# A gated mix of full and windowed attention on one core: shifted copies in place, four quads under way, and a new planner table

## The chip, the cores and the metric

The kernel runs on one core of a Trainium2 chip. The metric is the device time of one execution in microseconds (us); the median of three runs of the kernel before is 827.52 us. The core has five engines that work side by side, each through its own instructions in a fixed order, with semaphores between them: TensorE (PE in the profile) multiplies matrices, VectorE (DVE), ScalarE (ACT) and GpSimd (POOL) work on elements, and SyncE (SP) starts most transfers.

## The reference, cut to what matters

```python
x = A_x                                        # 1 x 2048 x 640, bf16
g = sigmoid((x * gate_w).sum(-1, keepdims=True))
# A: full attention, 32 heads of 20 columns
p = softmax(einsum("bhqd,bhkd->bhqk", q, k) * 20 ** -0.5)
a = einsum("bhqk,bhkd->bhqd", p, v)            # heads side by side, then @ A_wo
# B: each query sees 8 keys, at distances 0, 2, ..., 14
b = ...                                        # softmax over the 8, values, @ B_wo
return g * a + (1 - g) * b
```

q, k and v of A and of B are x times their own 640 x 1920 weights. The exponentials of A are the large work: 32 heads of 2048 x 2048 scores.

## The kernel before, in words

**Units, groups, tiles.** A *unit* is the scores of one head for 128 keys and 512 queries. A *group* is four heads (j = 0 to 3) and 512 queries, so 64 units, and there are 32 groups. Units come in *tiles*, numbered s. `next_tile` (L1472) puts two units in a tile, in one of two double-buffered score tensors, and a third if the third bank of that score tensor is free. That bank (x = 1 + s % 2) is also one of the three banks (`BANKS`, L342) in which all other PE work leaves its results, called `side`. `qk(s)` (L1511) makes the scores, with four heads in the four row strips of the array; `exp(s)` (L1544) lets ScalarE take the exponential of the two or three units into one of five buffers `ebuf`; `pv` (L1556) multiplies them by the values, four at a time in the four column strips, and adds up in one accumulator, `obank`, which serves one group after another. When a group's units are all added, `close` (L1635) starts its normalization (`gen_norm`).

**Rides and quads.** ScalarE doesn't take every unit. A unit can *ride* in the third place of a tile to VectorE, which makes a bit pattern of its exponential by arithmetic on integers (L1537: add an offset, clamp at 0, write int16, which is read as bf16). Four units of one key block, one of each head of a group, are a *quad*. To be exact enough, a quad is used four times, k = 0 to 3: as it is, and with 32, 64 and 96 added to its integers (`SHIFTS`, L48; the shift is L806), each time with values that have been multiplied by another weight (`WEIGHTS`; POOL does it once for a quad, L798, into `vS`). So a quad has four *slices*, and each slice has one value matmul for each head (L1592). In this kernel the quads lie in two buffers `uD`, and the shifted copies in a ring of three, `eD`.

**The planner.** All instructions are placed when the kernel is built. `_Sched.task` (L188) appends an instruction to its engine's list and charges it a duration; an engine's list runs in that order on the chip, and the charges decide only the order. A charge for signals (`LAT`) and one for a change between row strips and column strips (`SWITCH`) are added. The main loop (L1699 to 1753) makes for each tile s: scores, exponential, perhaps value matmuls (`pv_slot`, L1653), and then, in `spend`, side work until shortly before the charged end of the exponential before (`SLACK`). Side work is written as generators that ask for PE time, VectorE time or a bank, each with a priority (`step`, L1150): projections of q, k, v, the window attention of B (`gen_bproj`, `gen_b`), normalization, output (`gen_fold`), and the shifts (`gen_d`, L789). Where PE has too little to do, `filler` (L1599) adds matmuls on zeros or into a free bank.

**What holds rides and shifts back.** `wanted` (L1398) opens a quad only if its `uD` buffer is free, if no more than two quads have slices left, if VectorE's charged backlog is small, and if the group has at least `DTIME` left; a ride is taken only if the backlog is under `DWAIT`. `gen_d` shifts one quad after another, and only when a place of the ring is free. Slices are taken in order of quads and of k, up to three (`NS`) at a visit of `pv_slot`; it is visited at every second tile, or when two slices are ready. At a group's end `pv_slot` forces what is missing.

`PLAN` (L50) sets 18 such numbers anew from given tiles on. The pace of B is given by constants (`BT0`, `BT1`, `BALL`, `XT0`, `XT1`), which the change doesn't touch.

Of the kernel before, what the change touches and what calls it, by code (L numbers as in the profile page):

```python
# [50 lines left out]
    0: ((0.3, 0.64), 0.31, 2.5, 2.5, 0.49, -1.34, -0.1, 11.8, 7.0, 8.15, 0.52, 0.47, 4.4, 4.0, 0.0, 0.71, 2, 0.0),  # L51
    10: ((0.3, 0.64), 0.31, 2.5, 2.5, 0.66, -1.34, -0.1, 11.8, 7.0, 8.15, 0.52, 0.47, 4.4, 4.0, 0.0, 0.71, 2, 0.0),
    20: ((0.3, 0.64), 0.31, 2.5, 2.5, 0.49, -1.34, -0.83, 11.8, 7.0, 8.15, 0.52, 0.47, 4.4, 4.08, 0.0, 0.71, 2, 0.0),
    30: ((0.32, 0.68), 0.31, 2.5, 5.5, 0.94, -1.34, -0.83, 11.8, 7.0, 7.65, 0.52, 0.47, 4.4, 5.28, 0.0, 0.73, 2, 0.0),
    40: ((0.32, 0.68), 0.3, 2.5, 5.5, 0.94, -1.34, -0.83, 11.8, 7.0, 8.82, 0.52, 0.47, 4.4, 5.28, 0.0, 0.73, 2, 1),
    50: ((0.32, 0.81), 0.3, 2.5, 5.5, 0.94, -1.34, -0.83, 11.8, 7.0, 8.82, 0.52, 0.47, 4.4, 5.28, 0.0, 0.73, 2, 1),
    60: ((0.32, 0.68), 0.31, 2.5, 5.5, 0.94, -1.34, -0.83, 11.8, 6.7, 7.65, 0.52, 0.64, 4.4, 4.34, 0.0, 0.73, 2, 0),
    70: ((0.32, 0.68), 0.3, 2.5, 5.5, 0.94, -1.5, -0.83, 11.8, 5.5, 8.82, 0.52, 0.47, 4.76, 5.28, 0.0, 0.73, 2, 1),
    80: ((0.29, 0.82), 0.3, 2.5, 5.5, 0.94, -1.34, -0.83, 11.8, 7.0, 8.82, 0.52, 0.47, 4.4, 5.28, 0.0, 0.73, 2, 1),
    90: ((0.29, 0.82), 0.06, 2.5, 6.6, 0.95, -1.34, -0.83, 11.59, 7.0, 8.82, 0.52, 0.47, 4.4, 5.28, 0.0, 0.73, 2, 0),  # L60
    100: ((0.32, 0.68), 0.31, 2.5, 5.5, 0.94, -1.34, -0.83, 11.8, 7.0, 7.03, 0.52, 0.47, 4.4, 4.3, 0.0, 0.69, 2, -3),
    110: ((0.32, 0.68), 0.31, 2.5, 5.5, 0.94, -1.49, -0.5, 11.8, 7.0, 6.64, 0.52, 0.47, 4.4, 4.3, 0.0, 0.66, 2, -3),
    120: ((0.32, 0.68), 0.31, 5.5, 5.5, 0.94, -1.15, -0.5, 9.67, 7.0, 6.64, 0.52, 0.47, 4.4, 3.98, 0.0, 0.66, 2, -3),
    130: ((0.32, 0.68), 0.31, 2.5, 5.5, 0.82, -1.6, -0.5, 11.8, 7.0, 6.64, 0.52, 0.44, 4.4, 4.54, 0.0, 0.66, 2, 0),
    160: ((0.31, 0.76), 0.33, 2.5, 1.0, 0.82, -1.6, -0.34, 11.8, 7.0, 6.64, 0.61, 0.44, 4.4, 4.12, 0.0, 0.66, 2, 0),
    180: ((0.31, 0.76), 0.28, 2.5, 1.0, 0.72, -1.6, -0.5, 11.8, 5.5, 6.64, 0.52, 0.44, 4.4, 3.94, 0.0, 0.66, 2, 0),
    190: ((0.31, 0.76), 0.28, 2.5, 5.5, 0.72, -1.6, -0.5, 11.8, 5.5, 6.64, 0.52, 0.59, 3.16, 3.94, 0.0, 0.66, 2, 0),
    200: ((0.32, 0.68), 0.38, 2.5, 2.5, 0.94, -1.48, -0.65, 14.9, 7.0, 6.07, 0.52, 0.47, 4.4, 5.28, 0.0, 0.73, 1, -3),
    210: ((0.29, 0.69), 0.31, 2.5, 5.5, 0.94, -1.49, -0.5, 11.8, 7.0, 7.54, 0.67, 0.62, 4.4, 4.3, 0.0, 0.66, 1, -3),
    230: ((0.29, 0.69), 0.38, 2.5, 5.5, 0.94, -1.49, -0.5, 11.8, 7.0, 7.54, 0.67, 0.51, 4.4, 4.3, 0.0, 0.8, 2, -3),  # L70
    240: ((0.29, 0.69), 0.19, 2.5, 5.5, 1.12, -1.49, -0.5, 11.8, 7.0, 7.54, 0.7, 0.55, 4.4, 3.84, 0.0, 0.7, 2, -3),
    250: ((0.29, 0.69), 0.28, 2.5, 5.5, 0.94, -1.49, -0.5, 11.8, 7.0, 7.54, 0.67, 0.62, 3.7, 4.3, 0.0, 0.69, 2, -3),
    260: ((0.36, 0.63), 0.38, 2.5, 2.5, 1.09, -1.48, -0.65, 9.61, 7.0, 6.07, 0.52, 0.47, 4.4, 5.28, 0.0, 0.73, 1, -3),
    270: ((0.29, 0.69), 0.24, 2.5, 5.5, 0.94, -1.29, -0.5, 11.74, 7.0, 7.54, 0.67, 0.62, 3.7, 4.3, 0.0, 0.72, 2, -3),
    300: ((0.29, 0.69), 0.24, 2.5, 5.5, 0.94, -1.29, -0.33, 11.74, 7.0, 7.54, 0.67, 0.62, 3.7, 4.3, 0.0, 0.72, 2, -3),
    310: ((0.29, 0.69), 0.27, 1.0, 6.6, 0.94, -1.6, 0.4, 11.8, 5.5, 6.93, 0.67, 0.54, 4.85, 4.42, 0.0, 0.66, 1, -3),
    320: ((0.29, 0.69), 0.27, 1.0, 6.6, 0.94, -1.5, 0.17, 9.99, 7.0, 8.58, 0.67, 0.54, 4.85, 5.04, 0.0, 0.66, 1, -3),
    330: ((0.37, 0.63), 0.24, 1.0, 5.5, 0.94, -1.29, -0.5, 11.74, 7.0, 7.54, 0.67, 0.62, 3.7, 4.3, 0.0, 0.71, 2, -3),
    340: ((0.29, 0.69), 0.16, 2.5, 2.5, 0.94, -1.37, 0.35, 12.91, 7.0, 7.54, 0.6, 0.62, 5.69, 4.65, 0.0, 0.72, 2, -3),
    360: ((0.29, 0.69), 0.32, 2.5, 5.5, 0.94, -1.25, 0.28, 11.3, 6.7, 7.78, 0.6, 0.62, 4.87, 3.21, 0.0, 0.72, 2, -3),  # L80
    380: ((0.29, 0.69), 0.24, 2.5, 1.0, 0.94, -1.29, 0.35, 11.3, 7.0, 9.58, 0.43, 0.43, 4.87, 4.3, 0.0, 0.72, 2, -3),
    390: ((0.29, 0.69), 0.24, 2.5, 5.5, 0.94, -1.29, 0.35, 11.3, 7.0, 9.58, 0.6, 0.62, 4.87, 4.37, -0.24, 0.84, 2, -3),
    400: ((0.32, 0.66), 0.25, 2.5, 2.5, 0.94, -1.37, 0.35, 12.77, 7.0, 6.11, 0.6, 0.62, 5.69, 4.87, 0.0, 0.72, 1, -3),
    410: ((0.3, 0.61), 0.25, 1.0, 2.5, 0.94, -1.38, 0.35, 12.77, 7.0, 6.11, 0.6, 0.62, 5.69, 4.87, 0.0, 0.72, 1, -3),
    420: ((0.34, 0.65), 0.25, 2.5, 2.5, 0.94, -1.37, 0.35, 12.67, 7.0, 7.4, 0.6, 0.62, 5.69, 4.3, 0.0, 0.73, 1, -3),
    430: ((0.32, 0.66), 0.25, 2.5, 2.5, 0.94, -1.41, 0.35, 10.51, 5.5, 7.99, 0.6, 0.62, 5.69, 4.87, 0.12, 0.72, 1, -3),
    440: ((0.32, 0.66), 0.25, 2.5, 2.5, 0.94, -1.37, 0.4, 13.22, 7.0, 7.57, 0.6, 0.62, 5.69, 3.69, 0.0, 0.72, 1, -3),
    450: ((0.3, 0.63), 0.25, 2.5, 2.5, 0.94, -1.37, 0.26, 7.4, 5.5, 6.11, 0.6, 0.67, 5.56, 5.42, -0.14, 0.61, 1, -3),
    490: ((0.28, 0.56), 0.25, 2.5, 6.6, 0.94, -1.46, 0.26, 7.4, 5.5, 6.11, 0.6, 0.73, 5.84, 5.55, -0.14, 0.61, 2, -3),
    500: ((0.3, 0.63), 0.25, 2.5, 6.6, 0.94, -1.46, 0.26, 7.4, 5.5, 6.11, 0.6, 0.62, 5.84, 4.93, -0.14, 0.61, 1, -1.5),  # L90
    510: ((0.3, 0.63), 0.24, 5.5, 6.6, 0.94, -1.37, 0.4, 7.8, 5.5, 6.29, 0.6, 0.67, 5.56, 5.93, -0.02, 0.6, 1, -3),
    530: ((0.3, 0.63), 0.07, 2.5, 2.5, 0.94, -1.06, 0.05, 7.4, 5.5, 8.96, 0.6, 0.67, 4.4, 5.42, -0.14, 0.61, 1, -1.5),
    540: ((0.34, 0.55), 0.35, 1.0, 6.6, 1.32, -1.37, 0.36, 13.82, 7.0, 10.51, 0.58, 0.73, 6.26, 4.87, -0.08, 0.65, 2, -3),
    550: ((0.34, 0.55), 0.35, 1.0, 6.6, 1.32, -1.37, -0.85, 13.82, 7.0, 10.51, 0.27, 0.73, 6.26, 5.26, -0.08, 0.65, 1, -3),
    560: ((0.3, 0.63), 0.07, 2.5, 2.5, 1.39, -1.06, 0.05, 7.4, 5.5, 8.96, 0.6, 0.67, 4.4, 5.42, -0.14, 0.69, 1, -3),
    570: ((0.3, 0.63), 0.07, 2.5, 2.5, 1.39, -1.06, 0.05, 7.4, 5.5, 8.84, 0.6, 0.67, 4.4, 5.42, -0.14, 0.69, 1, -3),
    580: ((0.33, 0.51), 0.25, 1.0, 5.5, 0.87, -1.26, -0.43, 13.15, 7.0, 7.41, 0.7, 0.51, 6.5, 4.87, -0.17, 0.67, 1, -3),
    590: ((0.33, 0.51), 0.25, 1.0, 5.5, 0.84, -1.37, -0.5, 12.77, 7.0, 7.41, 0.58, 0.51, 6.31, 4.87, -0.17, 0.67, 1, -3),
    600: ((0.33, 0.51), 0.25, 1.0, 5.5, 0.84, -1.37, -0.5, 12.77, 7.0, 7.41, 0.58, 0.51, 6.31, 4.87, -0.17, 0.67, 1, 1),
    620: ((0.3, 0.64), 0.32, 2.5, 2.5, 0.49, -1.0, 0.02, 11.8, 7.0, 7.2, 0.52, 0.47, 4.4, 4.0, 0.0, 0.85, 2, 0),  # L100
    630: ((0.33, 0.51), 0.25, 1.0, 5.5, 0.84, -1.47, -0.5, 12.41, 7.0, 7.41, 0.58, 0.51, 6.31, 4.87, -0.1, 0.67, 1, 1),
    640: ((0.3, 0.64), 0.32, 2.5, 1.0, 0.49, -0.36, -0.1, 11.8, 7.0, 11.41, 0.52, 0.47, 4.4, 4.0, -0.11, 0.6, 2, -3),
    650: ((0.33, 0.51), 0.25, 5.5, 5.5, 0.84, -1.37, -0.5, 12.77, 7.0, 7.41, 0.58, 0.45, 6.31, 4.87, -0.22, 0.67, 1, 1),
    680: ((0.33, 0.51), 0.25, 5.5, 5.5, 0.84, -1.37, -0.5, 12.77, 7.0, 7.41, 0.58, 0.45, 6.31, 4.24, -0.28, 0.67, 1, 1),
    690: ((0.37, 0.55), 0.24, 5.5, 2.5, 0.84, -1.37, -0.01, 12.77, 7.0, 7.41, 0.58, 0.45, 6.31, 4.87, -0.22, 0.67, 1, 0),
    700: ((0.33, 0.51), 0.25, 5.5, 5.5, 0.92, -1.32, -0.5, 12.77, 7.0, 7.41, 0.58, 0.45, 6.23, 4.15, -0.22, 0.67, 1, 1),
    710: ((0.37, 0.45), 0.22, 6.3, 6.6, 0.84, -1.37, -0.88, 12.77, 6.2, 7.19, 0.58, 0.46, 6.31, 4.87, -0.22, 0.65, 1, 1),
    720: ((0.46, 0.47), 0.22, 6.3, 6.6, -0.02, -1.37, -0.88, 12.77, 5.5, 7.19, 0.58, 0.46, 6.31, 4.87, -0.22, 0.65, 1, 0),
}
WEIGHTS = (1.0, 0.83984375, 0.70703125, 0.59375)  # L110
# [218 lines left out]
def _build(ctx, nc, A_x, A_wqkv, A_wo, B_wqkv, B_wo, gate_w, out):  # L329
# [459 lines left out]
    def gen_d(d):  # L789

        n = len(ridden[d])
        while d > 0 and not done.get(("dq", d - 1)):
            yield ("cond",)
# [993 lines left out]
```

## Time and profile before

| | |
|---|---|
| three runs, device time | 827.09, 827.52, 828.34 us |
| the profiled execution, from its first to its last instruction | 826.0 us |
| ScalarE busy | 800.2 us in 763 instructions |
| TensorE matmuls busy | 775.0 us in 12387 |
| VectorE busy | 679.2 us in 1191 |
| GpSimd busy | 140.7 us in 194 |
| moved by DMA | 29.12 MB, of which read from HBM 11.94 MB |

The profile's span is 1.5 us under the median of the runs; what the prediction works out for the span is moved to the runs by that difference. Busy time is the union of an engine's records. A record of VectorE or ScalarE overlaps the next one by something like 0.1 to 0.2 us, so the price of an instruction in a row is the distance of two starts, not the length of a record. Records of matmuls overlap too, four at a time. A group's line reads: line of the kernel, engine, operation, output and inputs with their shapes, count, then busy time, mean record in ns, and the engine's idle time just before these instructions with what ended it.

### The profile page before, as it was taken

How to read it: one execution, taken by the hardware profiler on the slowest of the kernel's cores; microseconds unless marked ns; L12 is line 12 of the kernel's file. 1: busy time of each engine (PE TensorE's matmuls, PEld its weight loads, DVE VectorE, ACT ScalarE, POOL GpSimd, SP SyncE). 2: the span in 40 equal slices, each digit the busy share in tenths (PEclk: the TensorE clock that was granted, in tenths of full speed). 3: DMA queues.
4: the chain of work that ended last, by engine and by line, in shares of the span. 5: the costliest groups of instructions: out<-in, count | busy, mean ns of one | idle time of the engine just before them, and what ended most of it. 6: DMA issues, size and time to landing. Idle time of an engine off the chain costs nothing.

```text
span 826.0 us, 29186 instructions
## 1 busy us (share of the span) xinstructions
PE 775.0 (94%) x12387; PEld 281.2 (34%) x12389; DVE 679.2 (82%) x1191; ACT 800.2 (97%) x763; POOL 140.7 (17%) x194
## 2 busy tenths in 40 slices
PE   8999999999999999999999998899999999998898
PEld 5332222333333332333244233333333433343223
DVE  7667788789989878887898989898887977889973
ACT  4999999999999999999999999999999999999995
POOL 5022111630211111021201111111021111101210
PEclk9999999999999999999999999999999999999999
DMA  9112210200111110011001011100111011100000
GB/s 310 37 32 51 47 36 18 72 20 16 37 34 28 27 29 21 7 40 35 18 18 42 21 21 40 33 22 7 34 30 28 6 39 32 35 7 21 22 6 35
DMA packets 45014, 29.12 MB, mean 35 GB/s; under 512 B 27204, under 2 KB 43684, under 8 KB 44884
## 3 DMA queue, kind: packets, MB, share of 16 engines
q1 hardware_dynamic: 44596, 26.92, 12.5%
q8 instruction: 98, 1.61, 0.8%
q10 hardware_dynamic: 288, 0.33, 0.1%
q14 instruction: 32, 0.26, 0.1%
HBM read 11.94 MB, written 2.62 MB: 18 GB/s over the span
## 4 chain that ended last, share of the span: by engine, by line
ACT 52%; PE 25%; issue 20%; DVE 3%; ACTq 0%; DVEq 0%
ACT ebuf L1547 51%; PE score L1524 8%; PE obank L1592 5%; PE side L566 5%; PE score L566 4%; DVE uD L1537 1%; PE score L1239 1%; PE obank L468 1%; DVE eD L806 1%; ACT eB L923 0%; PE obank L1613 0%; PE side L1262 0%; ACT tB L957 0%; PE score L1613 0%; ACTq L285 0%
## 5 line engine op out<-in xcount | busy, mean ns | idle before, releaser
L1547 ACT ACTIVATE ebuf<-score 128x1024 bf16<-128x1024 f32 (+1 forms) x731 | 789.3, 1275 | 6.7 <-PE score L1524 5.7
L1524 PE MATMUL score<-qT,kT 32*128 32x512 bf16 x2048 | 290.5, 384 | 34.1 <-ACT ebuf L1547 25.7
L1537 DVE TENSOR_SCALAR uD<-score 128x512 int16<-128x512 f32 x324 | 216.1, 682 | 41.3 <-PE score L1524 38.4
L806 DVE TENSOR_SCALAR eD<-uD 128x2048 int16<-128x2048 int16 x243 | 169.0, 725 | 4.8 <-PE obank L1592 4.1
L1524 PEld LDWEIGHTS score<-qT,kT 32*128 32x128 bf16 x2048 | 71.6, 91 | 282.0 <-ACT ebuf L1547 202.9
L1592 PE MATMUL obank<-ebuf,vA 128*21 128x512 bf16 x1724 | 160.3, 385 | 2.4 <-ACT ebuf L1547 1.7
L798 POOL TENSOR_TENSOR vS<-vA,vw 128x252 bf16<-128x252 bf16 x81 | 62.0, 767 | 313.2 <-PE obank L1592 279.6
L566 PE MATMUL side<-xT,kvw 128*32 128x256 bf16 (+1 forms) x2540 | 102.6, 280 | 1.8 <-DVE rQ L960 0.6
L1592 PE MATMUL obank<-eD,vS 128*21 128x512 bf16 x972 | 83.4, 379 | 0.2 <-DVE eD L806 0.2
L566 PEld LDWEIGHTS side<-xT,kvw 128*32 128x32 bf16 x2540 | 59.5, 96 | 34.4 <-issue 17.9
L1592 PEld LDWEIGHTS obank<-ebuf,vA 128*21 128x21 bf16 x1724 | 37.9, 89 | 87.9 <-issue 70.3
L773 POOL TENSOR_TENSOR rcp<-rcp,gA 128x16 f32<-128x16 f32 x31 | 8.8, 283 | 279.2 <-DVE rcp L771 279.2
L979 DVE TENSOR_TENSOR stage<-qkvB,repB 128x1280 bf16<-128x1280 bf16 x64 | 52.8, 849 | 0.0
L878 DVE TENSOR_TENSOR stage<-qkvB 128x1280 bf16<-128x1280 bf16 x64 | 52.6, 847 | 0.2
L566 PE MATMUL side<-stage,ident 128*32 128x512 bf16 (+1 forms) x736 | 47.9, 349 | 1.7 <-DVE dst L670 0.9
L862 DVE CAST qkvB<-side 128x512 bf16<-128x512 f32 (+1 forms) x72 | 41.9, 591 | 8.8 <-PE side L566 8.6
L779 POOL TENSOR_TENSOR oN<-oTt,rcp 128x512 bf16<-128x512 f32 x31 | 33.0, 1064 | 2.4
L767 DVE STREAM_TRANSPOSE oTt<-obank 128x512 f32<-128x512 f32 x32 | 22.8, 711 | 11.4 <-PE obank L1592 10.8
L1592 PE MATMUL obank<-uD,vA 128*21 128x512 bf16 x324 | 31.5, 379 | 0.0
L1592 PEld LDWEIGHTS obank<-eD,vS 128*21 128x21 bf16 x972 | 23.5, 91 | 16.1 <-DVE eD L806 1.4
L1613 PE MATMUL obank<-xT,zero 128*32 128x512 bf16 x296 | 26.6, 384 | 0.0
L566 PE MATMUL side<-woA_d,oTd 128*32 128x512 bf16 (+2 forms) x520 | 26.0, 295 | 0.0
(169 smaller groups left out, 543.1 us busy)
## 6 DMA issues: line engine op xcount, KB each, us to landing
repB<-eB SPq DMA_DIRECT2D x128, 32.0 KB
WqP<-in_A_wqkv_dram SPq DMA_DIRECT2D x16, 160.0 KB
stage<-in_B_wqkv_dram SPq DMA_DIRECT2D x1, 2400.0 KB
oTd<-oN SPq DMA_DIRECT2D x108, 20.0 KB
qT<-dst SPq DMA_DIRECT2D x104, 20.0 KB
out_dram<-outsb SPq DMA_DIRECT2D x12, 160.0 KB
kvw<-in_A_wqkv_dram SPq DMA_DIRECT2D x2, 800.0 KB
oTd<-in_A_x_dram SPq DMA_DIRECT2D x2, 640.0 KB
```

The costliest lines, as they stand in the source:

```text
L566: ins = e.matmul(o[j:k, :], l(j) if callable(l) else l[:, j:k], r, start=(first and i == 0), stop=(last and i == n - 1), skip_group_check= ...
L779: T(en, c2, lambda e: e.tensor_tensor(oo, ii, ib, ALU.mult), reads=["rcp", "oTt"], writes=["oN0"])
L798: T("pool", 0.7, lambda e: e.tensor_tensor(vS[:, d % 2, :, :], _ap(vA, (kb * NQ + q) * 4 * DV, [[0, K - 1], [1, 4 * DV]]), _ap(vw, 0, [[1, ...
L806: T("dve", 0.11 + 0.1334 * n, lambda e, k=k, sl=sl: e.tensor_scalar(eD[:, sl % NS, 0:512 * n].bitcast(I16), uD[d % 2][:, 0:512 * n].bitcas ...
L862: t = TB(dvc(n * TOK), lambda e, o=o, i=i: e.tensor_copy(o, i), reads=[("side", b)], writes=[key])
L878: TB(dvc(CN * TOK, 2), lambda e, w=w, ks=ks: e.tensor_tensor(prodB(w), qB[:, :, :], ks, ALU.mult), reads=["qB", "kB"], writes=[("prod", w) ...
L979: TB(dvc(CN * TOK, 2), lambda e, w=w, vs=vs, rr=rr: e.tensor_tensor(prodB(w), vs, rr, ALU.mult), reads=["vB", ("repB", w4 % NR)], writes=[ ...
L1524: ins = e.matmul(o, kT[32 * j:32 * j + 32, q, kb * P:(kb + 1) * P], qT[g % NQT][32 * j:32 * j + 32, :], start=True, stop=True)
L1537: t = T("dve", 0.69, lambda e: e.tensor_scalar(uD[d % 2][:, 512 * i:512 * (i + 1)].bitcast(I16), side[x], UOFF, 0.0, op0=ALU.add, op1=ALU. ...
L1547: exps[s] = T("act", actc(512 * n), lambda e: e.activation(ebuf[s % NE][:, 0:512 * n], score[s % 2][:, 0:512 * n], ACTF.Exp, scale=LN2 / S ...
L1592: ins = e.matmul(obank[32 * j:32 * j + DV, :], v, src, start=(kb == 0), stop=(last and k >= len(lst) - 4), skip_group_check=True)
L1613: ins = e.matmul(o[32 * j:32 * j + 32, :], w[:, 32 * j:32 * j + 32] if best else w[:, :], xT[:, 0, 0:512], start=bool(best), stop=bool(bes ...
```

## The change

The planner's rules, its charges and its table change; so each engine's order does, and how many units ride.

- **Shifts in place.** `eD` goes. A shift adds 32 to the quad's own buffer, and it waits until the matmuls of the slice before it are done (`done["pk", d, k - 1]`). There are five `uD` buffers (`NU`) and three `vS` (`NVS`); the bytes of the five are those of the two and the ring.
- **Quads under way.** `wanted` opens a quad while no more than `MAXQ` + 1 have slices left (the table gives 3 nearly everywhere, here and there 1, 2 or 4), and quads are shifted side by side, not one after another.
- **Slices in any order of quads.** `pv_slot` takes at most one slice of each quad, from any quad of the group whose next slice is ready, up to three (`NPS`).
- **Visits.** Value matmuls are made at any tile at which `PVMIN` units wait (4 nearly everywhere, 8 for tiles 30 to 49) or two slices are ready.
- **Banks.** A generator gets a bank only if the time it says it needs (1.08 us, or 0.12 in one place), times `BNEED`, is left before the limit of this stretch.
- **Charges.** A copy of a ride 0.69 becomes 0.60; a shift 0.11 + 0.1334 n becomes 0.066 + 0.1334 n; the fixed part of VectorE's work 0.10 becomes 0.066, of ScalarE's 0.08 becomes 0.05; matmuls and signals change by a few ns.
- **Table.** `PLAN` has new values, with three more numbers in each row (`BNEED`, `PVMIN`, `MAXQ`), a row for nearly every five tiles up to tile 500, and that row from there on; before, rows went on to tile 720.

```diff
-LAT = {"pe": 0.22, "act": 0.18, "dve": 0.13, "pool": 0.15, "sp": 0.1}
-SWITCH = 0.11
+LAT = {"pe": 0.222, "act": 0.165, "dve": 0.135, "pool": 0.15, "sp": 0.1}
+SWITCH = 0.105
...
-    uD = [sb([P, 4 * 512], BF16, "uD%d" % i) for i in range(2)]
+    NU = 5
+    NVS = 3
+    uD = [sb([P, 4 * 512], BF16, "uD%d" % i) for i in range(NU)]
-    NS = 3
-    eD = sb([P, NS, 4 * 512], BF16, "eD")
...
-    mmc = lambda n: max(n, 64) / 2400.0 + 0.004
-    dvc = lambda n, mode=1: 0.10 + n * 1.0417e-3 / mode
-    actc = lambda n: 0.08 + n * 0.8334e-3
+    mmc = lambda n: max(n, 64) / 2400.0 + 0.006
+    dvc = lambda n, mode=1: 0.066 + n * 1.0417e-3 / mode
+    actc = lambda n: 0.05 + n * 0.8334e-3
...
     def gen_d(d):
-        while d > 0 and not done.get(("dq", d - 1)):
-            yield ("cond",)
-        while cur["pv"] < d - 1 or not done.get(("v", kb, q // 4)) or not done.get("vw"):
+        while d >= NVS and not done.get(("pk", d - NVS, K - 1)) or not done.get(("v", kb, q // 4)) or not done.get("vw"):
             yield ("cond",)
...
-            while npv[0] <= sl - NS:
+            while not done.get(("pk", d, k - 1)):
                 yield ("cond",)
-            yield ("dve", DAHEAD, sch.free(("eD", sl % NS)))
-            T("dve", 0.11 + 0.1334 * n, lambda e, k=k, sl=sl: e.tensor_scalar(
-                eD[:, sl % NS, 0:512 * n].bitcast(I16), uD[d % 2][:, 0:512 * n].bitcast(I16), SHIFTS[k], None, op0=ALU.add),
+            yield ("dve", DAHEAD, sch.free(*keys))
+            T("dve", 0.066 + 0.1334 * n, lambda e, k=k: e.tensor_scalar(
+                uD[u][:, 0:512 * n].bitcast(I16), uD[u][:, 0:512 * n].bitcast(I16), SHIFTS[k] - SHIFTS[k - 1], None, op0=ALU.add),
+              reads=keys, writes=keys, port=True)
...
+            if not force and now + BNEED * req[1] > limit:
+                return False
...
-            if ulock[len(dquads) % 2] or len(dquads) > cur["pv"] + 1 or now < D0 or not (
+            if ulock[len(dquads) % NU] or len(dquads) > cur["pv"] + MAXQ or now < D0 or not (
...
-            t = T("dve", 0.69, lambda e: e.tensor_scalar(
+            t = T("dve", 0.6, lambda e: e.tensor_scalar(
...
-        while not first and cur["pv"] < len(dquads) and dquads[cur["pv"]][0] == pvg and len(slices) < NS:
-            d, k = cur["pv"], cur["k"]
-            if not closed[d]:
+        for d in range(cur["pv"], len(dquads)):
+            if first or dquads[d][0] != pvg or len(slices) == NPS:
                 break
...
-        if s >= hold and (s % 2 == 0 or not acting or slices_ready() >= 2):
+        if s >= hold and (pv_ready() >= PVMIN or not acting or slices_ready() >= 2):
```

## The prediction

> **What bounds the kernel now.** I began with the busy table of the page, to see which engine is full.
>
> ```profile
> ## 1 busy us (share of the span) xinstructions
> PE 775.0 (94%) x12387; PEld 281.2 (34%) x12389; DVE 679.2 (82%) x1191; ACT 800.2 (97%) x763; POOL 140.7 (17%) x194
> ```
>
> ScalarE (ACT) is busy all but 26 us. The busy time by stages says where those 26 us lie: in columns, PE, PEld, DVE, ACT, POOL.
>
> ```profile
> 0.00:25.00 25.00, 22.43 (x242) 12.31 (x244) 17.96 (x45) 12.66 (x14) 12.27 (x21) 1.00 0.86 281
> 25.00:800.00 775.00, 730.52 (x11717) 260.24 (x11713) 651.55 (x1132) 771.45 (x735) 128.42 (x173) 1.00 0.11 28
> 800.00:826.00 26.00, 22.00 (x444) 8.65 (x436) 9.67 (x17) 16.12 (x16) 0.00 (x0) 0.99 0.08 27
> ```
>
> In the 775 us between, ACT lacks 3.5 us and VectorE (DVE) 123. The granted clock is 1.00. So the middle ends when ACT has done its exponentials, and it gets shorter only by giving ACT fewer of them. The groups by line, shapes kept apart, say what they are.
>
> ```profile
> L1547 ACT ACTIVATE ebuf<-score 128x1024 bf16<-128x1024 f32 x469 | 454.8, 1114 | 3.6 <-PE score L1524 3.2
> L1547 ACT ACTIVATE ebuf<-score 128x1536 bf16<-128x1536 f32 x262 | 370.5, 1562 | 3.1 <-PE score L1524 2.6
> L1537 DVE TENSOR_SCALAR uD<-score 128x512 int16<-128x512 f32 x324 | 216.1, 682 | 41.3 <-PE score L1524 38.4
> L806 DVE TENSOR_SCALAR eD<-uD 128x2048 int16<-128x2048 int16 x243 | 169.0, 725 | 4.8 <-PE obank L1592 4.1
> ```
>
> There are 2048 units (128 keys by 512 queries of a head). ACT does 469*2 + 262*3 = 1724 in 731 tiles, and 324 ride to DVE, which copies each (L1537) and shifts each four of them three times (L806). Since records overlap, the price is the distance of starts, and the chain that ended last gives it in order of time (start, length, what):
>
> ```profile
> 359.12 0.88 ACT ebuf L1547
> 360.00 0.02 issue
> 360.02 0.97 ACT ebuf L1547
> ...
> 379.38 1.26 ACT ebuf L1547
> 380.64 0.07 issue
> 380.71 1.23 ACT ebuf L1547
> ```
>
> A tile of two units takes 0.90 us and one of three 1.33. So a unit costs ACT 0.43 and a tile 0.05 besides: 469*0.90 + 262*1.33 = 771 us. On DVE the timeline shows
>
> ```profile
> 443.01 1.89 DVE L806 TENSOR_SCALAR eD<-uD 128x2048 int16<-128x2048 int16 x3
> ...
> 467.58 1.87 DVE L1537 TENSOR_SCALAR uD<-score 128x512 int16<-128x512 f32 x3
> ```
>
> that is (1.89-0.68)/2 = 0.60 from shift to shift, and the same for a copy. Last, DVE's waits: it stands idle not for lack of time but because the next copy's scores have not been made.
>
> ```profile
> DVE uD L1537 <- PE score L1524: 38.4, 69, 2.1
> ...
> DVE eD L806 <- PE obank L1592: 4.1, 9, 1.6
> ```
>
> **The new charges.** The planner fixes each engine's order by its own charges, so a charge decides what it believes to be free. Old against measured: a copy 0.69 (0.60), four units' shift 0.11 + 0.53 = 0.64 (0.60), an exponential 0.08 + 0.85 = 0.93 (0.90). The new ones give 0.60, 0.60 and 0.90. The old plan thought DVE fuller than it was by 324*0.09 + 243*0.04 = 39 us, and ACT by 731*0.03 = 22 us. The edit executes nothing; it offers up to 39 us more of DVE to rides. Its price lies in lost slack: a plan without margin that is late on DVE holds the bank of that ride, which the next tile but one needs.
>
> **Shifts in place, five buffers.** Before, at most two quads were under way, and only one was being shifted, into a ring of three. Now a shift overwrites the quad, and the next waits for the value matmuls of the slice before it. Count and size of shifts and matmuls per quad stay: three shifts and four slices. The wait added stands in DVE's queue ahead of copies and of the sliding-window work. The trace of before has no large shift in place. Its nearest wait is the ring's, 4.1 us for 243 shifts; if every shift paid the worst one of 1.6 us it would be 389 us, but the planner issues a shift only when it has planned the matmuls as done. Below: the ring's 4.1 us goes. I take 5 us, all of it in DVE's idle time. POOL's multiplication (L798, 0.6 us) is done once for each quad, as before.
>
> **Four quads under way.** Its worth is work for DVE in the 38 us of L1537's waits and in the other gaps. The price of one ride in records is 216.1/324 + 169.0/243*3/4 = 0.67 + 0.52 = 1.19 us of DVE's busy time. If r more units ride, ACT is 0.43 r shorter, and DVE has 651.6 + 1.19 r of 775 - 0.43 r to do. The bounds are r = 0 (the table allows no more) and DVE full: 123.4/1.62 = 76. In its best stretches before, DVE reached 94%:
>
> ```profile
> 450.00:475.00 25.00, 24.38 (x375) 8.14 (x369) 23.57 (x37) 25.00 (x24) 3.81 (x5) 1.00 0.10 25
> ```
>
> I take that as its mean, because several quads give it something to do in nearly every gap: 0.94*(775 - 0.43 r) = 651.6 + 1.19 r gives r = 48, thus 93 quads for 81, and ACT loses 48*0.43 = 20.6 us.
>
> Shifts also share something with POOL. Of the 243, the longest took 1.805 us, the median 0.683, the mean 0.725: 10 us of excess, beside POOL's work. At that mean, 36 more shifts cost 1.5 us of DVE, about one ride, 0.4 us of the end. The Trainium skill, SBUF — State Buffer, section Who interferes with whom, says more: a VectorE operation that uses two ports and a GpSimd operation lock each other out of a shared pair for the whole instruction. By that rule each of the 12 new multiplications could hold a shift for its whole 0.6 us, an estimate of 7 us of DVE or 6 rides, 2.5 us of the end; the long records beside POOL agree with the rule, but most shifts escape, so the sum goes by the mean.
>
> **Banks only with time left; value matmuls at any visit.** Of 731 tiles, 731 - 324 - 262 = 145 had only two units, because side work held the third bank. With p such tiles there are (2048 + p)/3 tiles. A side group that cannot run before the next tile no longer takes a bank, so p falls; bounds are 0 (683 tiles, 48*0.05 = 2.4 us of ACT) and 200 (749 tiles, 0.9 us lost). I take p = 100: 716 tiles, 0.8 us gained. Value matmuls at any visit change no count; they come earlier, which frees buffers, at one more change of kind on PE (0.1 us) where a tile had no such work. PE takes both: r = 48 adds 144 units of value matmuls, 36 packs of four at about 0.21 = 7.7 us, and 15 tiles fewer take off 15*0.21 = 3.2 us. PE still has filler (L1613, 536 matmuls, 134 packs, 28 us) and its waits on ACT (25.7 us). If that cover is gone, those 4.5 us are ACT's.
>
> **The table.** It executes nothing itself. Its last row holds from tile 500 of some 716, so the last 30% run under one setting. The fixed pace of the sliding-window work (170 of its charge by 905) stays, while the new charges make that work about 160: the planner sees it behind sooner, so the tail, in which its last output lies at 798 of 826, keeps its length. Bounds for this part: 5 us either way; I take nothing.
>
> **Sum.** 826.0 - 20.6 - 0.8 = 804.6 for the profiled span; the median of the runs, 827.5, is 1.5 above the span, so 806.
>
> **Rivals.**
> - *DVE gets nearly full.* At 97% r = 62, 26.7 us, and p = 60 another 1.4: 799.4. With 100%, r = 76 and no two-unit tile: 792. For it: with several quads under way a shift or a copy is at hand for most gaps. Against it: the normalization's waits (L767, 10.8 us; L781, 8.2) are no free gaps.
> - *Only part comes.* The table's conditions let few more ride; r = 20 gives 8.6 us, thus 819; r = 0 leaves 827.
> - *Slower: late quads at the ends of groups.* One accumulator serves the 32 groups in turn, so a group's last slices must be done before the next group's value matmuls start. In the ring three shifts of a late quad run in 1.89 us without PE between them. In place each takes a round trip: 0.68 for the shift, 0.39 for the matmuls and the planner's 0.14 + 0.22 for the signals, 1.4 each, 4.3 for three, 2.4 more. Five buffers of exponentials, two always in use, cover three tiles, some 3.2 us; from the point at which the last slice is later than that behind the last scores, ACT stops. A mean of 1 us over that point in each of 32 groups costs 32 us and turns 806 into 838. Against it: the table opens no quad with less than about 11 us left.
> - *Shifts in place run at a lower rate.* Its record of 0.68 us for 2048 elements against 0.69 for a reduction of 512 (L606) shows that the shift moves about four elements in the time of one. If in place it fell to two, a shift would take about 1.1 us: 243*0.5 = 122 us on DVE, and DVE, with 651.6 + 122 of 775, would end the run; with 48 rides more, at 1.57 each, 849 of busy time plus the 51 us of start and tail is 900. The Trainium skill, VectorE: DVE Perf Modes, section Mode 2×_2P — use both read ports for one tensor, warns of an output that overlaps its input there, since the second port starts half-way. It speaks of partial overlap, and here each element is written where it was read. No run here shows it.
>
> **Chances.** The forecast (800 to 812) has 0.48; fuller (below 800) 0.13; part (812 to 826) 0.14; no change 0.05; late quads (829 to 850, likeliest 838) 0.17; a lower rate (900) 0.03. Faster by over 0.2% (1.7 us, about what a measurement of this kernel can tell from no change) is 0.75, slower 0.20. The range of 8 in 10 leaves out the fullest cases below 793 and most of the late quads above 832.
>
> **What would show it.** Right: L1537 some 372 times and the shifts some 279, each shift still near 0.68 by median; some 716 tiles; DVE above 90% in the middle, ACT as full as now. Wrong: as many rides as before; ACT's waits on L1524, now 5.7 us, at 20 or more, with value matmuls waiting for shifts at the ends of groups; shifts of 1.1 us; or a tail of more than 26 us after the last ride.

## The result, and the profile after

The changed kernel takes 835.97 us (median of 4 runs, 834.55 to 837.54) against 827.85 for the kernel before: a ratio of 1.0096, 95% interval 1.0084 to 1.0108. It is slower by 1%, outside the predicted range and on the other side. The profiled execution spans 835.7 us. Busy time of the changed kernel, from its page:

```profile
## 1 busy us (share of the span) xinstructions
PE 778.0 (93%) x12105; PEld 277.0 (33%) x12105; DVE 697.9 (84%) x1233; ACT 791.6 (95%) x759; POOL 140.9 (17%) x200
...
ACT  4999999999999999999999999999899998999990
...
PEclk9999999999999999999999999999999998998689
```

ACT has 8.6 us less to do in a span 9.7 us longer, so it is not its work that grew. The last two rows are 40 slices of the span: ACT has a nearly empty last slice, and the granted TensorE clock, in tenths of full speed, falls near the end. The groups, shapes kept apart:

```profile
L1586 ACT ACTIVATE ebuf<-score 128x1024 bf16<-128x1024 f32 x479 | 468.6, 1093 | 12.2 <-PE score L1563 11.6
L1586 ACT ACTIVATE ebuf<-score 128x1536 bf16<-128x1536 f32 x247 | 354.5, 1521 | 3.5 <-PE score L1563 3.3
...
L1576 DVE TENSOR_SCALAR uD<-score 128x512 int16<-128x512 f32 x348 | 233.9, 682 | 48.3 <-PE score L1563 46.5
L845 DVE TENSOR_SCALAR uD<-uD 128x2048 int16<-128x2048 int16 x261 | 180.7, 711 | 11.8 <-PE obank L1627 11.3
```

Of the units 348 ride, 24 more, in 727 tiles (one more tile has a single unit). ACT now waits 11.6 us for the scores of two-unit tiles, where it was 3.2. Its waits, for whom, in total, times, longest; first the changed kernel, then the kernel before:

```profile
ACT stage L1129 <- PE side L1110: 15.5, 1, 15.5
ACT ebuf L1586 <- PE score L1563: 14.9, 20, 2.0
```

```profile
ACT stage L1091 <- PE score L1072: 6.2, 1, 6.2
ACT ebuf L1547 <- PE score L1524: 5.7, 8, 2.0
```

Two waits grew, by 9 us each: one wait for the last matmuls of the run, and many small ones for scores.

**Where the small ones are.** Busy time and clock by stages (PE, PEld, DVE, ACT, POOL, clock, share of DMA, GB/s) at the same times of both executions, the changed kernel and then the kernel before:

```profile
340.00:400.00 60.00, 56.68 (x931) 20.20 (x928) 51.17 (x90) 58.17 (x58) 9.35 (x14) 0.94 0.10 26
575.00:600.00 25.00, 21.22 (x330) 7.84 (x326) 20.92 (x39) 22.64 (x22) 1.94 (x3) 0.93 0.08 19
675.00:725.00 50.00, 44.21 (x759) 16.82 (x751) 40.49 (x74) 47.44 (x45) 7.08 (x12) 0.93 0.13 33
750.00:800.00 50.00, 42.23 (x508) 11.61 (x500) 39.55 (x67) 46.51 (x43) 7.54 (x9) 0.80 0.07 17
400.00:575.00 175.00, 167.29 (x2792) 61.40 (x2788) 159.30 (x278) 174.94 (x169) 25.98 (x41) 1.00 0.11 26
```

```profile
340.00:400.00 60.00, 56.04 (x957) 20.90 (x949) 50.06 (x88) 60.00 (x57) 7.38 (x12) 1.00 0.10 26
575.00:600.00 25.00, 23.78 (x436) 8.95 (x428) 21.38 (x40) 24.89 (x29) 0.62 (x1) 1.00 0.12 33
675.00:725.00 50.00, 47.94 (x781) 15.88 (x778) 38.61 (x66) 49.93 (x45) 6.81 (x11) 1.00 0.12 34
750.00:800.00 50.00, 44.56 (x625) 13.64 (x621) 43.61 (x73) 49.88 (x49) 8.11 (x11) 1.00 0.08 20
```

In these four stages, in which the clock is under 1, ACT lost 1.8 + 2.3 + 2.5 + 3.4 = 10 us more than before; in the 175 us between the first two, at full clock, nothing. The clock is recorded as 0.5 in pieces of 3.41 us or a multiple, eight of them before the end (the eighth, at 801.7, lies behind these stages). Of the 13.8 us in which ACT has no record ahead of an exponential (the first left out), 9.1 lie within such a piece or in the 4 us behind it. At the change from one group to the next, where late quads would show, there is one wait of 1.8 us.

**The filler.** PE's matmuls on zeros or into a free bank, the changed kernel and the kernel before:

```profile
L1648 PE MATMUL obank<-xT,zero 128*32 128x512 bf16 x88 | 7.9, 397 | 0.0
L1648 PE MATMUL side<-xT,ident 128*32 128x512 bf16 x60 | 6.1, 462 | 0.0
L1648 PE MATMUL score<-xT,ident 128*32 128x512 bf16 x32 | 3.0, 384 | 0.2 <-ACT ebuf L1586 0.2
```

```profile
L1613 PE MATMUL obank<-xT,zero 128*32 128x512 bf16 x296 | 26.6, 384 | 0.0
L1613 PE MATMUL score<-xT,ident 128*32 128x512 bf16 x140 | 12.3, 381 | 0.0
L1613 PE MATMUL side<-xT,ident 128*32 128x512 bf16 x100 | 7.4, 382 | 0.0
```

180 matmuls, 45 packs of four, where 134 packs had been: the table's `FILL`, the load under which `filler` adds a pack, is 0.42 to 0.63 in most rows from tile 110 on, where it had been 0.6 to 0.85. No run here changes `FILL` alone; that it took the packs away is read from the table.

**The tail.** The last exponential starts at 815.0 (814.2 before). What PE does after it, from the timeline of the changed kernel (start, length, what):

```profile
816.23 1.37 PE L607 MATMUL side<-woA_d,oTd 128*32 128x512 bf16 x20
817.53 3.64 PE L607 MATMUL score<-stage,ident 128*32 128x512 bf16 x64
821.00 1.04 PE L607 MATMUL side<-stage,ident 128*32 128x256 bf16 x32
822.58 0.46 PE L607 MATMUL score<-woBp,oB 128*32 128x128 bf16 x20 [0.53 <-DVE oB L1034]
...
829.18 1.36 PE L607 MATMUL score<-woA_d,oTd 128*32 128x512 bf16 x20
830.47 0.41 PE L1110 MATMUL score<-outsb,oN 128*32 128x128 bf16 x16
```

`stage,ident` is the summation of the last piece of B. Its output used to be ready at 798 (L996), now at 822 (L1034), and the output projections that need it follow. The two lines, the changed kernel and then the kernel before (count, shortest, median and longest record in ns, first and last start in us):

```profile
L1034 DVE SCALAR_TENSOR_TENSOR oB<-side,rB x22: 406/676/692, 241.0 to 822.1; 128x512 bf16<-128x512 f32 x14, 128x256 bf16<-128x256 f32 x8
```

```profile
L996 DVE SCALAR_TENSOR_TENSOR oB<-score,rB x1: 423/423/423, 797.9 to 797.9; 128x256 bf16<-128x256 f32 x1
```

**One account for all runs.** A tile of two units costs ACT 0.904 us from start to start, of three 1.331 and of one 0.48; the sum is ACT's work on exponentials. From the first start to the last end, what is beyond the work is called idle time here. It is not all waiting: some 5 us of it, in every run, are ACT's 20 other instructions, gaps without a record are 4.7 us in the kernel before and 13.8 in the changed one, and the rest are starts that lie a little further apart. The tail is from the last end to the end of the span.

| kernel | rides | work | idle | tail | span | clock | median |
|---|---|---|---|---|---|---|---|
| before | 324 | 772.7 | 22.9 | 10.9 | 826.0 | 1.000 | 827.9 |
| changed | 348 | 762.2 | 33.7 | 20.3 | 835.7 | 0.975 | 836.0 |
| changed, filled | 348 | 762.2 | 24.5 | 20.4 | 826.0 | 0.999 | 827.6 |
| before, thin filler | 324 | 772.7 | 33.5 | 10.9 | 835.9 | 0.971 | 836.8 |
| changed, later rows | 340 | 765.8 | 29.4 | 11.9 | 825.7 | 0.987 | 828.3 |
| later rows, filled | 340 | 765.8 | 22.3 | 11.9 | 819.4 | 1.000 | 820.9 |
| before, filled | 324 | 772.7 | 23.9 | 11.2 | 826.8 | 0.999 | 828.4 |
| later rows, 45 packs | 340 | 765.8 | 23.5 | 11.9 | 820.8 | 0.997 | 822.5 |
| rows from 400 on, filled | 340 | 765.8 | 22.2 | 10.5 | 817.1 | 1.000 | 819.3 |
| two quads, filled | 248 | 804.8 | 32.2 | 10.8 | 867.5 | 0.997 | 868.1 |
| no bank rule, filled | 324 | 773.2 | 57.5 | 13.9 | 863.3 | 0.999 | 866.9 |

So the change does take 10.5 us of work from ACT, loses 10.8 to idle time, and adds 9.4 of tail: 9.7 in all.

### The profile page after: what moved, and what is told of

The parts are those of the page before. It is cut to its first block, busy times and chain, and to the rows that moved or that the text cites. A ratio compares the mean times of both kernels' runs of the same rounds, so it can differ in the third digit from the quotient of the medians.

```text
span 835.7 us, 28717 instructions
## 1 busy us (share of the span) xinstructions
PE 778.0 (93%) x12105; PEld 277.0 (33%) x12105; DVE 697.9 (84%) x1233; ACT 791.6 (95%) x759; POOL 140.9 (17%) x200
## 4 chain that ended last, share of the span: by engine, by line
PE 43%; ACT 36%; issue 16%; DVE 5%; ACTq 0%; DVEq 0%
ACT ebuf L1586 36%; PE score L1563 13%; PE obank L1627 11%; PE side L607 11%; PE score L607 4%; DVE uD L845 1%; DVE uD L1576 1%; DVE stage L1017 1%; PE score L1280 1%; DVE stage L916 1%; PE obank L509 1%; PE side L1648 0%; ACT eB L961 0%; PE obank L1648 0%; PE side L1303 0%
## 5 line engine op out<-in xcount | busy, mean ns | idle before, releaser
L1586 ACT ACTIVATE ebuf<-score 128x1024 bf16<-128x1024 f32 (+1 forms) x727 | 779.6, 1238 | 15.8 <-PE score L1563 14.9
L1563 PE MATMUL score<-qT,kT 32*128 32x512 bf16 x2048 | 297.3, 392 | 44.2 <-ACT ebuf L1586 39.3
L1576 DVE TENSOR_SCALAR uD<-score 128x512 int16<-128x512 f32 x348 | 233.9, 682 | 48.3 <-PE score L1563 46.5
L845 DVE TENSOR_SCALAR uD<-uD 128x2048 int16<-128x2048 int16 x261 | 180.7, 711 | 11.8 <-PE obank L1627 11.3
L1627 PE MATMUL obank<-ebuf,vA 128*21 128x512 bf16 x1700 | 170.3, 395 | 3.1 <-DVE oTt L808 1.9
L607 PE MATMUL side<-xT,kvw 128*32 128x256 bf16 (+1 forms) x2310 | 97.7, 286 | 2.1 <-DVE qkvB L900 0.8
L1627 PE MATMUL obank<-uD,vS 128*21 128x512 bf16 x1044 | 96.9, 394 | 0.2 <-DVE uD L845 0.2
L900 DVE CAST qkvB<-side 128x512 bf16<-128x512 f32 (+1 forms) x64 | 37.0, 588 | 4.0 <-PE side L607 3.7
L1627 PEld LDWEIGHTS obank<-uD,vS 128*21 128x21 bf16 x1044 | 24.9, 92 | 9.5 <-issue 2.9
L808 DVE STREAM_TRANSPOSE oTt<-obank 128x512 f32<-128x512 f32 x32 | 22.7, 708 | 5.9 <-PE obank L1627 5.9
L607 PE MATMUL side<-woBp,oB 128*32 128x512 bf16 (+1 forms) x480 | 25.5, 314 | 0.0
```

The lines of the kernel that those rows point to most:

```text
L607: ins = e.matmul(o[j:k, :], l(j) if callable(l) else l[:, j:k], r, start=(first and i == 0), stop=(last and i == n - 1), skip_group_check= ...
L808: T("dve", dvc(512), lambda e: e.transpose(oTt[:, :], obank[:, :]), reads=["obank"], writes=["oTt"])
L845: T("dve", 0.066 + 0.1334 * n, lambda e, k=k: e.tensor_scalar(uD[u][:, 0:512 * n].bitcast(I16), uD[u][:, 0:512 * n].bitcast(I16), SHIFTS[k ...
L900: t = TB(dvc(n * TOK), lambda e, o=o, i=i: e.tensor_copy(o, i), reads=[("side", b)], writes=[key])
L1563: ins = e.matmul(o, kT[32 * j:32 * j + 32, q, kb * P:(kb + 1) * P], qT[g % NQT][32 * j:32 * j + 32, :], start=True, stop=True)
L1576: t = T("dve", 0.6, lambda e: e.tensor_scalar(uD[d % NU][:, 512 * i:512 * (i + 1)].bitcast(I16), side[x], UOFF, 0.0, op0=ALU.add, op1=ALU. ...
```

## The experiments

The theory after the result: the clock falls because fillers are missing (*clock*), and B's last piece is late (*tail*). The rival is that of the prediction, shifts in place that come late and hold up ACT (*chain*). Since a changed number of the table changes every order behind it, the fillers were tried with all orders kept.

**Packs in the planned waits of the changed kernel.** After all is placed, a pack of four zero matmuls goes into each 0.25 us of a planned wait of PE of 0.3 us or more, wherever `obank` is adding up:

```diff
...
+            gap = sch.busy[i][0] - lst[i - 1].end if i else 0.0
+            if safe[i] and gap >= 0.3:
+                for _ in range(int(gap / 0.25)):
+                    new.append(_Task(-1, "pe", "cmp", one, []))
...
```

> The changed kernel in its own order, plus 160 packs of four zero matmuls in the places where PE is planned to wait. Theory clock (the new table asks for a third of the fillers, PE's activity falls too low in some stretches, the clock is halved there and ACT waits for scores): the clock stays at 1.00, ACT's waits on the scores fall from 14.9 us to some 6, and the median falls from 836 to about 825. Theory chain (ACT waits because shifts in place come late at the ends of groups): the clock may be whole, but the time stays at 836 +- 2, since no shift comes earlier.

Measured: 827.63 us, ratio to the kernel before 0.9998 (0.9989 to 1.0008), so 8.3 us are back, 2.6 fewer than expected. ACT's waits:

```profile
ACT stage L1129 <- PE side L1110: 15.6, 1, 15.6
ACT ebuf L1586 <- PE score L1563: 7.7, 10, 2.1
```

The wait for scores is halved and the one in the tail is as it was. No order was changed, the one wait at a group's end is still 1.8 us, and yet the idle time fell by 9.2: *chain* doesn't explain it.

**The opposite, on the kernel before.** The packs stay where they are, with 16 columns:

```diff
...
-                ins = e.matmul(o[32 * j:32 * j + 32, :], w[:, 32 * j:32 * j + 32] if best else w[:, :], xT[:, 0, 0:512], start=bool(best),
+                ins = e.matmul(o[32 * j:32 * j + 32, 0:16], w[:, 32 * j:32 * j + 32] if best else w[:, :], xT[:, 0, 0:16], start=bool(best),
...
```

> The kernel before in its own order, with each of its 134 filler packs cut from 512 columns to 16. Theory clock: the clock falls in several stretches as in the changed kernel (mean under 0.99), and the time rises from 827.5 to 835 to 850. Theory chain: fillers are of no use, the time is 827.5 or, with less on PE, 1 us less.

Measured: 836.75 us, 1.0106 (1.0093 to 1.0119): PE has less to do, nothing else differs, and the kernel before becomes as slow as the changed one. The clock by slices, and ACT's wait:

```profile
PEclk9999999999899999999999999999999999997599
```

```profile
ACT ebuf L1547 <- PE score L1524: 15.0, 23, 2.1
```

**Later rows of the table.** Rows for the tiles from 540 on are added, chosen so that in the plan B's window work ends some 20 us earlier. Up to there all orders are those of the changed kernel.

```diff
+    540: ((0.49, 0.5), 0.21, 1.0, 5.5, 0.52, -1.6, 0.37, 13.55, 7.0, 6.88, 0.6, 0.6, 5.11, 4.54, -0.09, 0.54, 2, 0, 0.23, 4.0, 3.0),
+    545: ((0.39, 0.84), 0.35, 5.5, 1.0, 0.83, -0.66, 0.13, 15.1, 6.7, 4.61, 0.51, 0.47, 4.28, 3.48, 0.29, 0.65, 2, 0, 0.0, 4.0, 3.0),
...
+    725: ((0.37, 0.61), 0.49, 5.5, 1.0, 0.64, -1.05, 0.59, 14.3, 7.0, 4.61, 0.54, 0.12, 4.37, 2.68, -0.05, 0.51, 2, 0, 0.23, 4.0, 3.0),
```

> The changed kernel, the same order up to tile 540, and other rows of the table after it, chosen so that the window work of B ends some 20 us earlier (340 rides instead of 348). Theory tail (the changed kernel loses 9 us because the last piece of B and the last output projections stand behind the last exponential): the stretch from the last exponential to the end falls from 20 us to about 11, the last exponential comes some 3 us later for 8 rides fewer, and the median is about 830; the clock still falls in places. Without that theory: 836 or more.

Measured: 828.27 us, 1.0002 (0.9993 to 1.001). The tail is 11.9, the work 3.6 more for 8 rides fewer. The idle time fell by 4 too, which was not expected: there are 55 packs instead of 45, and the clock's mean is 0.987.

**Both.** The later rows, and 117 packs by the rule above.

> Both edits, the later rows and 117 packs of zero matmuls in PE's planned waits. If clock and tail are two separate losses, both are gained: about 819, faster than the kernel before by 8 us. If one hides the other: no better than the better of the two alone, some 825.

Measured: 820.91 us, 0.9916 (0.9903 to 0.9929). The two losses are separate and together more than the whole loss.

```profile
PE 792.0 (97%) x12589; PEld 284.2 (35%) x12589; DVE 687.9 (84%) x1219; ACT 793.0 (97%) x761; POOL 137.8 (17%) x198
```

```profile
ACT stage L1152 <- PE score L1133: 7.0, 1, 7.0
...
ACT ebuf L1609 <- PE score L1586: 6.1, 8, 2.0
```

ACT's waits are those of the kernel before (6.2 and 5.7), with shifts in place and quads side by side as in the change. What is left is the 6.9 us of work that the rides take from ACT. No run here gives the kernel before newly chosen rows, so how much of this the changed rules could claim, and how much the choice of rows, is open.

**Control: packs in the kernel before.** The same insertion, 130 packs.

> Control: the kernel before in its own order, plus 130 packs of zero matmuls in PE's planned waits. Theory clock: its clock never falls, so there is nothing to gain, 827.5 +- 1. If the packs help by some other way (a warm weight path, a shorter start of the scores), it is 820 like the kernel with both edits, and then the gain there is not the change's own.

Measured: 828.35 us, 1.0006 (0.9997 to 1.0014). Where the clock doesn't fall, packs gain nothing, and they cost nothing that shows. The kernel before stands close to a fall, though: in 3 of the 17 runs measured beside this one its mean clock is 0.995 and its time 829.4 to 829.6, while all 11 runs with packs have 0.999 or more.

**Dose.** `gap >= 0.6` in place of 0.3, with the later rows: 45 packs.

> The changed kernel with the later rows and only 45 packs instead of 117, in planned waits of 0.6 us or more. Theory clock with a threshold (a stretch falls only if matmuls stream in less than some 45% of it, and those are the stretches with the longest waits): the few packs are enough, clock 1.00 and 821 +- 1. If each pack counts in proportion: halfway, some 825.

Measured: 822.45 us, 0.9926 (0.9909 to 0.9942), clock 0.997. Of the 7.4 us that 117 packs gain over none, 5.8 come with 45, so the longest waits count most. It is a little above the 821 +- 1 of a pure threshold: the clock still fell once before the end in the profiled run.

**Rows from tile 400 on.** Other rows from 400, found in the same way, with 106 packs.

> The changed kernel with other rows from tile 400 on (340 rides, 729 tiles, the last exponential planned 2.3 us earlier) and 106 packs. The accounting by ScalarE's work, its idle time and the tail says: the work is that of the run with both edits, the idle time 2 us less, so some 818. If the planner's small gains are lost in the real timing: 821, the same.

Measured: 819.32 us, 0.9894 (0.9881 to 0.9907), the fastest version here. Of the 2.3 us expected, 1.6 came, more in the tail (10.5) than in idle time.

**Two quads.** The changed kernel, with packs.

```diff
...
             FILL, HOLD, BOFF, BNEED, PVMIN, MAXQ) = plan
+            MAXQ = 1.0
...
```

> The changed kernel with MAXQ = 1 in every row, so that at most two quads have slices left as before, and packs in PE's planned waits to keep the clock; the rest of the table is as it was and not chosen for this. 248 units ride, 100 fewer than in the changed kernel. If the shifts in place keep a quad longer under way than the ring did, four quads mostly make up for that: by ScalarE's work, 762 us plus 100 x 0.43 = 805, plus some 24 idle, 19 before and 10 after, it is some 860. If ScalarE no longer set the end (DVE or PE did), fewer rides would cost less: under 845.

Measured: 868.1 us, 1.0484 (1.0466 to 1.0503); the account said 860, with 24 idle where it was 32. DVE's groups show where its time went:

```profile
L1576 DVE TENSOR_SCALAR uD<-score 128x512 int16<-128x512 f32 x248 | 168.1, 685 | 67.7 <-PE score L1563 66.3
...
L845 DVE TENSOR_SCALAR uD<-uD 128x2048 int16<-128x2048 int16 x186 | 129.4, 716 | 32.5 <-PE obank L1627 32.3
```

Shifts wait 32.3 us for PE (11.3 with up to four quads, 4.1 with the ring), and copies 66.3. Under the same limit of two quads the ring had 324 rides and shifts in place have 248. The other numbers of the table were chosen with `MAXQ` = 3, so the 76 can't be laid to shifts in place alone. That much of what four quads bring is spent on the longer life of a quad fits these waits, but is not shown.

**Banks at any time.** The changed kernel, with packs.

```diff
...
             FILL, HOLD, BOFF, BNEED, PVMIN, MAXQ) = plan
+            BNEED = 0.0
...
```

> The changed kernel with BNEED = 0 in every row, so that side work takes a bank at any time, and the packs; the rest of the table unchanged. 324 units ride in 742 tiles. By ScalarE's work (772.7 us plus 11 tiles x 0.05 = 773.3) with 24 idle and 19 before: the last exponential at 817; the window work ends late, so a tail of some 18: 837 us. If the bank rule mattered for PE's side work more than for the tiles, ScalarE's idle time falls under 20 and the run is under 832.

Measured: 866.87 us, 1.0474 (1.0456 to 1.0491), missed by 30: the idle time is 57.5, of which 38.6 are waits for scores. The work is as expected. Here *chain* is seen: ten of ACT's waits, 24.9 us together, end at the change from one group to the next, where the changed kernel has one of 1.8. PE at such a place:

```profile
473.39 0.40 PE L1627 MATMUL obank<-uD,vS 128*21 128x512 bf16 x4 [0.16 <-DVE uD L845]
474.61 0.61 PE L1627 MATMUL obank<-ebuf,vA 128*21 128x512 bf16 x8 [0.82 <-DVE oTt L808]
475.05 0.60 PE L1627 MATMUL obank<-uD,vA 128*21 128x512 bf16 x8
475.58 0.60 PE L1563 MATMUL score<-qT,kT 32*128 32x512 bf16 x5
```

A group's last slice waits for its shift (L845), the next group's value matmuls wait until the accumulator has been read (L808), and the scores stand behind both; ACT waits 3.2 us. Why the plan without the rule is so late with these slices, and whether rows chosen for it would do better, is open.

## Why the prediction was wrong

- *What bounds.* Right: ACT's work sets the middle, and its terms held. 24 rides and 4 tiles fewer give 24*0.43 + 4*0.05 = 10.5 by the prediction's prices; the account measures 10.5.
- *Four quads under way: r = 48.* Mis-sized: 24. The step that failed is the mean of 94% for DVE, taken from its best stretch. It was 661.67 of 775, 85%, and its waits for the next copy's scores grew from 38.4 to 46.5 us. The number of rides is fixed when the kernel is built, by the table's conditions, so DVE's room on the chip was no measure of it; in these runs more quads didn't make the scores come sooner. In the run with both edits it is 663.81, no more. What holds it there beyond that was not separated. With 24 rides and all else as forecast the time would have been some 816, which is the rival *only part comes*.
- *Shifts in place.* The rate was right: three shifts in the same 1.89 us as in the ring,

```profile
799.78 1.89 DVE L845 TENSOR_SCALAR uD<-uD 128x2048 int16<-128x2048 int16 x3
```

  so the rival of a lower rate is out; the median record is 0.683 us in both. The warning of the Trainium skill, VectorE: DVE Perf Modes, section Mode 2×_2P — use both read ports for one tensor, is of an output that partly overlaps its input; here, where the two coincide, no loss of rate shows. The wait is 11.3 us where 5 was taken, in DVE's idle time. The mean record, 725 ns before, is 711, so the shifts beside POOL's work cost less and not more.
- *Banks.* 133 third places left empty (3*727 - 2048) where 100 was taken: 727 tiles for 716, 0.6 us.
- *Filler as cover.* This failed, and with the next point it turned the sign. The prediction counted PE's 28 us of filler as time that other work may take, at no price, and wrote "the granted clock is 1.00" as a fact of the kernel. It was what the filler paid for: 10 us of idle time on ACT come with the clock (packs added: -9.2; packs thinned in the kernel before: +10.6).
- *The table: "I take nothing".* This failed too. It holds `FILL`, and it runs under one row from tile 500; the prediction named that row and still let the tail keep its length. It measured +9.4 us.
- *Lost slack of the new charges.* Not separated.
- *The rival that ended on the slower side,* late quads at the ends of groups, came out at the right size (838) for another reason. PE's waits on shifts are 1.1 us, and 11.6 in front of weight loads, but at the ends of groups ACT waited only 1.8 us, and with clock and tail mended its idle time is 22.3, as before. The mechanism itself exists: without the bank rule it takes 24.9 us.

## What to carry to other kernels

A filler, or any load that only keeps a unit awake, is not slack: before a plan takes it away, ask what it holds up, and read the granted clock beside the count. When the busiest engine gets less work, write three lines, its work, its idle time and the tail behind it, for each version; a gain in the first is easily eaten by the others, and each has its own cure. A table chosen along one course of a planner is tied to that course: try parts of such a change in the same order of instructions, or with rows chosen anew.

## What the runs showed of the hardware

The clock fell although matmuls were never absent for long: in the changed kernel the longest stretch without a matmul record, after the start, is 1.1 us; in the profiled execution of the kernel before, whose clock didn't fall, 1.3. What differs is the share. I laid stretches of 3.41 us on the recorded falls and summed the time in which a matmul streams (columns at 2.4 per ns, since two packs of 512 columns start 0.215 us apart at the closest; overlaps once): the stretch ahead of a fall has 0.31 to 0.44 in seven of eight cases in the changed kernel and 0.51 in one, while the emptiest stretch of the kernel before has 0.50 and of the filled one 0.50. Two stretches at 0.43 and 0.46 passed without a fall. In four other runs (thin filler, later rows, 45 packs, two quads) twelve falls have 0.30 to 0.49 ahead of them, and the emptiest stretch that passed has 0.44. So in these runs a fall came behind every full-clock stretch under 0.43 and behind none over 0.51, start and end left out; between the two both happened. That is an estimate from a modelled streaming time, not a rule. The Trainium skill, TensorE: Matmul & The Clock Gate, section HAM oscillation — how this bites in real kernels, asks that PE have no idle gap over about 3.4 us. By that rule alone no fall was to come here; the runs show eight without such a gap, so the measurement decides: keeping gaps short was not enough, and what went with the falls was a low share of streaming time. Where a fall comes isn't settled by the order alone: up to 608 us the changed kernel and the one with later rows have the same orders, with falls at 358, 392 and 587 us in the one and a single one, twice as long, at 356 in the other.
